# A one-token decode block on one core: the same tiles, written engine by engine with its own semaphores

## The chip, the cores and the metric

The kernel runs on one core of a Trainium2 chip. The metric is the device time of one execution in microseconds (us); less is better. The core has TensorE (PE, matrix products), VectorE (DVE), ScalarE (ACT), GpSimd (POOL) and SyncE (SP, which here issues every DMA), and 16 DMA engines that carry data from HBM into SBUF.

## What is computed

One layer of a transformer decodes one token for two sequences. Attention reads a cache of keys and values; a bilinear feed-forward part follows.

```python
B, Sq, D = 2, 1, 448
H, Sk, Dh = 16, 8192, 256          # heads, cached positions, dims of a head

q = (layernorm(x) @ wq) by heads                     # B, H, 1, Dh
scores = einsum("bhqd,bhkd->bhqk", q, k_cache) * Dh**-0.5
o = einsum("bhqk,bhkd->bhqd", softmax(scores), v_cache)
h = x + o @ wo
n = layernorm(h)
out = h + ((n @ w_gate) * (n @ w_up)) @ w_down       # F = 1792
```

All numbers are float32. The two caches are 2 x 16 x 8192 x 256 numbers each: 32 pairs of a head and a sequence (a *query* below), and for each query 8.39 MB of K and 8.39 MB of V. Each cached number is used once.

## The kernel before

**The work on a query.** `tile_decode_block` is written on a tile framework that places the semaphores: it loops over the 32 queries `i` (L312) in the order in which the program is written. For each it loads K as one tile of 128 partitions x 16384 numbers (`load_k`, L96 to L99) and V as another (`load_v`, L101 to L104). There is one buffer for K and there are two for V; the weight `wq` uses one of V's two first (L106). The scores `s` are four PSUM banks of 128 x 512: a partition group of 32 rows stands for a quarter of the positions.

**Scores, two ways** (`scores`, L253 to L278). The 256 dims of K lie in two halves. In 19 queries TensorE takes both halves, with 32 matmuls at L269. In the other 13 (`by_vector`, L47: every third query and the last three) TensorE takes the lower half with 16 matmuls, VectorE multiplies and adds the upper half (one `tensor_scalar` at L256, then four `scalar_tensor_tensor` at L261, the last two on half the columns each), and TensorE adds its result with 4 matmuls at L275. Then VectorE finds the maximum of each row (L322), and ScalarE makes `p = exp(s - max)` and its sums (L324).

**Values, two ways** (L343 to L352). `WIDE = (8, 8, 0)` says by `i % 3` how many of V's eight slices are taken together. In 19 queries VectorE multiplies all 128 x 16384 numbers of V by `p` (L346) and sums them (L347); in 13 it runs one `scalar_tensor_tensor` with a running sum on each of eight slices (L350).

**After the loop.** The softmax of a query is done piece by piece on 128 partitions, and `weights` (L280) works out the factors that put the pieces together: for the first 30 queries at the end of query 29, for the last two while the last V is on its way. `weigh` (L305) applies them. Then come the output projection (`project_out`, L390), the layer norm, the gate and up products (`project_ff`, L435), their product, the down projection (`add`, L460), two copies to SBUF and one DMA out (L477). The weights for this are loaded behind the last V through the same buffers: `wo` (L359), then gate, up and down in pieces (L366).

**What sets the order.** Every engine runs its instructions in the order of the program. SP's list is `wq`, K0, V0, K1, V1 and so on to V31 and then the weights; a DMA is issued when its buffer is free, and all of them share one queue. K(i+1) waits until TensorE and VectorE have read K(i). The framework has eight semaphores for DMA landings and uses them in turn. At its end (L541) it makes SP wait for every last count, joins all engines in a barrier, clears the semaphores on GpSimd and joins them again.

Of the kernel before, what the change touches and what calls it, by code (L numbers as in the profile page):

```python
# [1 line left out]

# [6 lines left out]
F32 = mybir.dt.float32  # L9
# [5 lines left out]
EPS = 1e-5  # L15
P = 128
HALF = 64
DC = 4
# [23 lines left out]


WIDE = (8, 8, 0)


def by_vector(i):  # L47
    return i % 3 == 0 or i >= NQ - 3

# [6 lines left out]

@with_exitstack
def tile_decode_block(  # L60
    ctx: ExitStack,
    tc: tile.TileContext,
    kc: bass.AP,
    vc: bass.AP,
    wq: bass.AP,
    wo: bass.AP,
    wg: bass.AP,
    wu: bass.AP,
    wd: bass.AP,
    out: bass.AP,  # L70
):

    nc = tc.nc
    const = ctx.enter_context(tc.tile_pool(name="const", bufs=1))
    kbuf = ctx.enter_context(tc.tile_pool(name="kbuf", bufs=1))
    vbuf = ctx.enter_context(tc.tile_pool(name="vbuf", bufs=2))
    one = ctx.enter_context(tc.tile_pool(name="one", bufs=1))
    work = ctx.enter_context(tc.tile_pool(name="work", bufs=2))  # L90
    ps_s = ctx.enter_context(tc.tile_pool(name="ps_s", bufs=1, space=bass.MemoryType.PSUM))
    ps_m = ctx.enter_context(tc.tile_pool(name="ps_m", bufs=2, space=bass.MemoryType.PSUM))
    ps_1 = ctx.enter_context(tc.tile_pool(name="ps_1", bufs=1, space=bass.MemoryType.PSUM))
    ctx.enter_context(tc.manual_schedule())

    def load_k(b, h):  # L96
        t = kbuf.tile([P, 2, G, GK], F32, tag="k", align_bytes=512, name=f"k_{h}_{b}")
        nc.sync.dma_start(t.rearrange("p c g k -> p (c g k)"), kc[b, h])  # L98
        return t  # L99

    def load_v(b, h):  # L101
        t = vbuf.tile([P, NO, GK], F32, tag="v", align_bytes=512, name=f"v_{h}_{b}")
        nc.sync.dma_start(t.rearrange("p o k -> p (o k)"), vc[b, h])
        return t  # L104

    wq_t = vbuf.tile([P, WQ + DC * B], F32, tag="v", align_bytes=512, name="wq_t")  # L106
    nc.sync.dma_start(wq_t, wq)  # L107

    ident = const.tile([P, P], F32, name="ident")
    make_identity(nc, ident)  # L110
    ones = const.tile([P, P], F32, name="ones")
    nc.gpsimd.memset(ones, 1.0 / R)
    eps_t = const.tile([P, 1], F32, name="eps_t")
    nc.gpsimd.memset(eps_t, EPS)
    gsum = const.tile([P, R], F32, name="gsum")
    xr = const.tile([P, DC + 1, B, 16], F32, name="xr")
    nc.gpsimd.memset(xr[:, DC - 1 :], 0.0)
    oT = const.tile([P, H, 2, B], F32, name="oT")
    block = const.tile([P, P], F32, name="block")
    nc.gpsimd.memset(block, 0.0)  # L120
    for g in range(G):
        nc.gpsimd.memset(block[g * R : (g + 1) * R, g * R : (g + 1) * R], 1.0)
    nm = const.tile([P, NQ], F32, name="nm")
    ls = const.tile([P, NQ], F32, name="ls")
    oacc = const.tile([P, NQ, NO], F32, name="oacc")
    acc_ps = ps_1.tile([P, D], F32, name="acc_ps")

    def clear(t):
        nc.scalar.activation(
            t, eps_t[: t.shape[0]].to_broadcast([t.shape[0], t.shape[1]]), AF.Copy, scale=0.0  # L130
        )

    clear(acc_ps)

    def over_chunks(t, tag):

        got = const.tile([P, B], F32, name=f"sum_{tag}")
        nc.vector.tensor_reduce(  # L138
            got, t[:, : DC - 1].rearrange("p c b -> p b c"), axis=AX.X, op=ALU.add
        )  # L140
        nc.vector.scalar_tensor_tensor(  # L141
            got, t[:, DC - 1, :], 0.5, got, op0=ALU.mult, op1=ALU.add
        )
        return got

    def center(h, tag):
        total = ps_m.tile([P, B], F32, tag="sm", name=f"total_{tag}")
        nc.tensor.matmul(total, ones, over_chunks(h, f"h_{tag}"), start=True, stop=True)  # L148
        if h.space == bass.MemoryType.PSUM:
            stays = const.tile([P, DC, B], F32, name=f"stays_{tag}")  # L150
            nc.scalar.activation(stays, h, AF.Copy)
            h = stays
        xc = const.tile([P, DC, B], F32, name=f"xc_{tag}")
        nc.vector.scalar_tensor_tensor(
            xc, total[:, None, :].to_broadcast([P, DC, B]), -R / D, h, op0=ALU.mult, op1=ALU.add
        )
        return xc

    def squares(xc, tag):
        sq = const.tile([P, DC, B], F32, name=f"sq_{tag}")  # L160
        nc.vector.tensor_mul(sq, xc, xc)
        return over_chunks(sq, f"sq_{tag}")

    xT = const.tile([P, DC, B], F32, name="xT")
    nc.scalar.activation(xT, wq_t[:, WQ:].rearrange("p (c b) -> p c b", c=DC), AF.Copy)  # L165
    xc = center(xT, "x")
    var = ps_m.tile([P, B], F32, tag="sm", name="var_x")
    nc.tensor.matmul(var, ones, squares(xc, "x"), start=True, stop=True)
    std = const.tile([P, B], F32, name="std")
    nc.scalar.activation(std, var, AF.Sqrt, bias=eps_t, scale=R / D)  # L170
    rstd = const.tile([P, B], F32, name="rstd")
    nc.vector.reciprocal(rstd, std)

    def spread_out(xc, by):

        for (rows, c, to), copy in zip(LAYOUT, by):
            k = rows.stop - rows.start
            copy(
                xr[rows, to],
                xc[rows, c][:, :, :, None].to_broadcast([k, c.stop - c.start, B, 16]),  # L180
            )

    def scalar_copy(to, x):
        nc.scalar.activation(to, x, AF.Copy)  # L184

    xn = const.tile([P, DC, B], F32, name="xn")
    nc.vector.tensor_mul(xn, xc, rstd[:, None, :].to_broadcast([P, DC, B]))
    spread_out(xn, (scalar_copy,) * 3)
    nc.vector.tensor_reduce(
        gsum, ident.rearrange("p (g r) -> p r g", r=R), axis=AX.X, op=ALU.add  # L190
    )

    def project(ps, w, size, wide, at0, at3):
        for c in range(DC):
            for g in range(4):
                xs = xr[:, c]
                at = c * size + at0[g]
                if c == DC - 1:
                    xs = xr[:, c + g % 2]
                    at = 3 * size + at3[g]  # L200
                nc.tensor.matmul(  # L201
                    ps[32 * g : 32 * g + 32, : wide[g]],
                    xs.rearrange("p b r -> p (b r)"),
                    w[:, at : at + wide[g]], start=(c == 0), stop=(c == DC - 1),
                )

    qT = const.tile([P, 2, G, 2, 2, B], F32, name="qT")
    q_ps = ps_s.tile([P, 4, MM], F32, tag="s", name="q_ps")
    q_sb = one.tile([P, 3, MM], F32, tag="p", name="q_sb")
    spread = q_sb[:, 2].rearrange("p (o g r) -> p o g r", o=G, g=G)  # L210
    nc.gpsimd.tensor_copy(
        spread,
        ident.rearrange("p (o r) -> p o r", r=R)[:, :, None, :].to_broadcast([P, G, G, R]),
    )
    for k in range(2):
        project(
            q_ps[:, k], wq_t, HD, (MM,) * 4, [k * BATCH + g * MM for g in range(4)],
            [k * BATCH // 2 + (g // 2) * MM for g in range(4)],
        )
        nc.scalar.activation(q_sb[:, k], q_ps[:, k], AF.Copy, scale=DH**-0.5)  # L220
        for n in range(4):
            nc.tensor.transpose(
                q_ps[:, 2 + k, n * P : (n + 1) * P], q_sb[:, k, n * P : (n + 1) * P], ident
            )
        nc.scalar.activation(
            qT[:, k].rearrange("p g j c b -> p (j c) g b"),
            q_ps[:, 2 + k].rearrange("p (n g b r) -> p n g b r", n=4, g=G, b=B)[..., 0],
            AF.Copy,
        )


    qd = const.tile([P, G, NQ], F32, name="qd")
    qd_ps = ps_m.tile([P, G, NQ], F32, tag="sm", name="qd_ps")
    for o in range(G):
        nc.tensor.matmul(
            qd_ps[:, o, :].rearrange("p (n b) -> p n b", b=B),
            spread[:, o].rearrange("p g r -> p (g r)"),
            qT.rearrange("p k g j c b -> p (k g j) c b")[:, :, 1, :],
            start=True, stop=True,
        )  # L240
    nc.scalar.activation(qd, qd_ps, AF.Copy)

    def queries(h):
        q = one.tile([P, 2, B, R], F32, tag="q", name=f"q_{h}")
        nc.scalar.activation(  # L245
            q.rearrange("p c b r -> p (c b) r"),
            qT.rearrange("p k g j c b -> p (k g j) (c b)")[:, h, :, None]
            .to_broadcast([P, 2 * B, R]),
            AF.Copy,
        )  # L250
        return q

    def scores(s, q, i, kt):  # L253
        upper = kt[:, 1]
        if by_vector(i):
            nc.vector.tensor_scalar(  # L256
# [288 lines left out]
```

## Time and profile before

| | us |
|---|---|
| median of 3 runs | 1303.92 |
| lowest and highest | 1303.84, 1303.94 |
| span of the profiled execution (first to last instruction) | 1302.1 |

The page gives no time of its own for the profiled execution beyond its span. The median of the runs is 1.8 us longer; that is what lies around the span, ahead of the first instruction and behind the last. The profiled execution's own time is therefore taken as 1302.1 + 1.8 = 1303.9.

How to read the rows. A row of a timeline says when something starts, how long it takes, on which engine, at which line, what it writes and reads, and in brackets how long the engine sat idle before it and what ended that. SPq rows are DMA issues; the transfer itself comes later. PE rows with "x32" may be fewer matmuls in the program: each float32 matmul is two passes there. PEclk is TensorE's granted clock as a share of 2.4 GHz.

### The profile page before, as it was taken

To read this page: it belongs to the slowest core of one execution; us is meant where nothing else is said; L and a number is where in the kernel's file an instruction comes from. 1 tells how busy PE (TensorE), PEld (TensorE's weight loads), DVE (VectorE), ACT (ScalarE), POOL (GpSimd) and SP (SyncE) were. 2 spreads that over 40 slices of the span, in tenths; PEclk is the share of its full clock that TensorE was granted. 3 is DMA by queue.
4 is the path that set the end of the run, shared out by engine and by line. 5 is a ranking of instruction groups with operands and counts; after the bars stand their busy time and mean duration, and the time that the engine had idled before them with its cause. 6 is when DMAs were issued, how large, how long until landed. Compare 5 with 4: busy or idle time off the path is not lost.

```text
span 1302.1 us, 5034 instructions
## 1 busy us (share of the span) xinstructions
PE 340.6 (26%) x2114; PEld 103.4 (8%) x2114; DVE 1075.6 (83%) x381; ACT 80.4 (6%) x111; POOL 2.2 (0%) x15
## 2 busy tenths in 40 slices
PE   2422112232202223211322311322311232221247
PEld 0100000000000000000000000000000000000013
DVE  0499879969987998899799879979987996987773
ACT  1100000000000000000000000000000000000000
POOL 0000000000000000000000000000000000000000
PEclk9866566666556666556666556666656666656668
DMA  9999999999999999999999999999999999999998
GB/s 419 419 449 421 447 423 445 425 443 427 439 429 441 425 441 427 437 428 437 433 435 433 434 435 435 435 433 437 431 439 431 437 429 435 433 433 433 433 425 358
DMA packets 11401, 561.50 MB, mean 431 GB/s; under 512 B 1266, under 2 KB 1652, under 8 KB 2292
## 3 DMA queue, kind: packets, MB, share of 16 engines
q1 hardware_dynamic: 11380, 561.20, 99.6%
q8 instruction: 16, 0.26, 0.1%
q14 instruction: 5, 0.04, 0.0%
HBM read 561.19 MB, written 0.00 MB: 431 GB/s over the span
## 4 chain that ended last, share of the span: by engine, by line
DMA 73%; PE 17%; DVE 10%; issue 1%; SPq 0%; DVEq 0%; ACT 0%; ACTq 0%
DMA k<-in_kc_dram 67%; PE s L269 13%; DVE k L261 6%; DMA v<-in_vc_dram 4%; PE s L275 3%; DVE v L350 3%; DMA wd_t<-in_wd_dram 2%; DVE k L256 1%; PE acc_ps L462 0%; SPq L366 0%; SPq L107 0%; PE u_ps L462 0%; SPq L98 0%; DVEq L256 0%; ACT tail L184 0%
## 5 line engine op out<-in xcount | busy, mean ns | idle before, releaser
L269 PE MATMUL s<-k,q 128*32 128x512 f32 x1632 | 248.3, 773 | 892.5 <-DMA k<-in_kc_dram 892.5
L346 DVE TENSOR_TENSOR v<-v,p 128x16384 f32<-128x16384 f32 x19 | 327.3, 17226 | 81.2 <-DMA v<-in_vc_dram 61.2
L347 DVE TENSOR_REDUCE oacc<-v 128x8 f32<-128x16384 f32 x19 | 327.2, 17220 | 0.7
L350 DVE SCALAR_TENSOR_TENSOR v<-v,p 128x2048 f32<-128x2048 f32 x104 | 231.1, 2288 | 31.8 <-ACT p L324 21.9
L269 PEld LDWEIGHTS s<-k,q 128*32 128x32 f32 x1632 | 66.7, 138 | 1070.9 <-issue 1069.2
L324 ACT ACTIVATE p<-s,nm 128x2048 f32<-128x2048 f32 x32 | 63.0, 1967 | 1131.7 <-DVE nm L322 1131.7
L322 DVE TENSOR_REDUCE nm<-s 128x1 f32<-128x2048 f32 x32 | 73.1, 2285 | 33.8 <-PE s L275 33.8
L261 DVE SCALAR_TENSOR_TENSOR k<-k,qd 128x2048 f32<-128x2048 f32 (+1 forms) x52 | 93.4, 1817 | 1.4
L275 PE MATMUL s<-k,block 128*128 128x512 f32 x104 | 48.1, 605 | 18.1 <-DVE k L261 18.1
L256 DVE TENSOR_SCALAR k<-k,qd 128x2048 f32<-128x2048 f32 x13 | 16.7, 1286 | 29.2 <-DMA k<-in_kc_dram 27.0
L275 PEld LDWEIGHTS s<-k,block 128*128 128x128 f32 x104 | 18.7, 189 | 49.0 <-DVE k L261 33.5
L138 DVE TENSOR_REDUCE sum_h_x<-xT 128x2 f32<-128x6 f32 x1 | 0.2, 159 | 20.6 <-ACT xT L165 20.6
L395 PE MATMUL acc_ps<-wo_t,oT 128*2 128x448 f32 x64 | 8.8, 646 | 11.4 <-DMA wo_t<-in_wo_dram 11.2
L201 PE MATMUL q_ps<-wq_t,xr 128*32 128x512 f32 x64 | 9.6, 753 | 1.4 <-ACT xr L184 1.1
L350 DVE DVE_READ_ACCUMULATOR v<-v,p 128x1 f32 x104 | 8.6, 83 | 0.0
L201 PE MATMUL ff_ps<-gu_t,xr 128*32 128x512 f32 (+1 forms) x32 | 6.4, 913 | 0.6 <-ACT xr L184 0.6
L324 ACT ACTIVATION_READ_ACCUMULATOR p<-s,nm 128x1 f32 x32 | 6.2, 193 | 0.0
L148 PE MATMUL total_x<-sum_h_x,ones 128*128 128x2 f32 x2 | 0.6, 348 | 21.1 <-DVE sum_h_x L141 21.1
L442 DVE TENSOR_SCALAR ve<-var_h 128x1 f32<-128x1 f32 x1 | 0.2, 158 | 6.4 <-PE var_h L440 6.4
L476 DVE COPY tail<-acc_ps 2x112 f32<-2x112 f32 x1 | 0.3, 261 | 5.5 <-PE acc_ps L462 5.5
L245 ACT ACTIVATE q<-qT 128x128 f32<-128x128 f32 x16 | 4.8, 298 | 0.0
L201 PE MATMUL u_ps<-gu_t,xr 128*32 128x512 f32 (+1 forms) x32 | 3.6, 544 | 0.0
(103 smaller groups left out, 66.0 us busy)
## 6 DMA issues: line engine op xcount, KB each, us to landing
wq_t<-in_wq_dram SPq DMA_DIRECT2D x1, 7172.0 KB, 19.6
wo_t<-in_wo_dram SPq DMA_DIRECT2D x1, 3584.0 KB, 16.5
wo_t<-in_wo_dram SPq DMA_DIRECT2D x1, 2688.0 KB, 22.5
gu_t<-in_B_w_gate_dram SPq DMA_DIRECT2D x1, 1792.0 KB, 28.0
gu_t<-in_B_w_up_dram SPq DMA_DIRECT2D x1, 1792.0 KB, 34.5
gu_t<-in_B_w_gate_dram SPq DMA_DIRECT2D x1, 1344.0 KB, 30.7
wd_t<-in_wd_dram SPq DMA_DIRECT2D x1, 1120.0 KB, 16.8
wo_t<-in_wo_dram SPq DMA_DIRECT2D x1, 896.0 KB, 24.2
```

The lines of the kernel that those rows point to most:

```text
L201: nc.tensor.matmul(ps[32 * g : 32 * g + 32, : wide[g]], xs.rearrange("p b r -> p (b r)"), w[:, at : at + wide[g]], start=(c == 0), stop=(c ...
L245: nc.scalar.activation(q.rearrange("p c b r -> p (c b) r"), qT.rearrange("p k g j c b -> p (k g j) (c b)")[:, h, :, None] .to_broadcast([P ...
L256: nc.vector.tensor_scalar(upper[:, 0], upper[:, 0], qd[:, 0, i : i + 1], None, op0=ALU.mult)
L261: nc.vector.scalar_tensor_tensor(upper[:, 0, at], upper[:, o, at], qd[:, o, i : i + 1], upper[:, 0, at], op0=ALU.mult, op1=ALU.add,)
L269: nc.tensor.matmul(s[g * R : (g + 1) * R, at], q[:, c, i % B, :], kt[:, c, g, at], start=(c == 0), stop=(c == 1), skip_group_check=True,)
L275: nc.tensor.matmul(s[:, at], block, upper[:, 0, at], start=False, stop=True, skip_group_check=True,)
L322: nc.vector.tensor_reduce(nm[:, i : i + 1], s, axis=AX.X, op=ALU.max, negate=True)
L324: nc.scalar.activation(p, s, AF.Exp, bias=nm[:, i : i + 1], scale=1.0, accum_out=ls[:, i : i + 1])
L346: nc.vector.tensor_mul(v, v, p[:, None, :].to_broadcast([P, n, GK]))
L347: nc.vector.tensor_reduce(oacc[:, i, :n], v, axis=AX.X, op=ALU.add)
L350: nc.vector.scalar_tensor_tensor(v, v, 1.0, p, op0=ALU.mult, op1=ALU.mult, accum_out=oacc[:, i, o : o + 1])
L395: nc.tensor.matmul(acc_ps[32 * j : 32 * j + B, :], oT[:, h, c, :], wo_t[:, k * D : (k + 1) * D], start=(h < 2 and j > 0), stop=(h >= H - 2 ...
```

## The change

The kernel is written again without the tile framework. Tiles are placed by hand at fixed addresses, each engine's list of instructions is written out, and the semaphores are the kernel's own. In front of and behind the loop a small class (`Flow`) keeps the last writer and the readers of each tile and emits a wait for each dependence. In the loop the waits are written by hand.

- **One form for all 32 queries.** VectorE always takes the upper half of K's dims, TensorE the lower; V is always taken in eight slices. The L346 and L347 forms are gone. The pieces, tiles and PSUM banks are as before, and so are all bytes loaded.
- **GpSimd hands landings over.** It waits for K's landing and increments `k_for_pe` and `k_for_dve`; it waits for V's and increments `v_for_dve`. TensorE and VectorE wait for these and set them back to zero (`take`). GpSimd also copies the query (`q_now`, `qd_now`) ahead of each K, and the eight sums of V (`oacc_now`) away behind each V. ScalarE copies the maximum away.
- **When K's buffer is taken again.** SP issues K(i+1) when VectorE has found the maximum of query i (`n_max`).
- **The end.** `weights` is done once for all 32 queries, between the eight slices of the last V; each load has a semaphore of its own; the matmuls that bring in `x` (L385) move ahead of the loop.
- **No closing barriers.** SP issues the output, clears the semaphores, and waits for the output's landing; nothing joins the engines.

```diff
+    def take(e, name):
+        f.engines[e].wait_ge(sem[name], 1).then_inc(sem[name], -1)
+
+    def pe_scores():
+        take("pe", "k_for_pe")
         for at in tiles:
...
+        for j, at in enumerate(tiles):
+            if j % 2 == 0:
+                take("pe", "part")
+            last = pe.matmul(
+                s[:, at], block, k_t[:, 1, 0, at], start=False, stop=True, skip_group_check=True
             )
+        last.then_inc(sem["scored"], 1)
...
+    def dve_scores():
+        take("dve", "k_for_dve")
...
+        take("dve", "scored")
+        dve.tensor_reduce(nm_now, s, axis=AX.X, op=ALU.max, negate=True).then_inc(sem["n_max"], 1)
...
+    def dve_values(j):
+        take("dve", "v_for_dve")
+        take("dve", "p_ready")
+        for o in range(NO):
+            last = mix(v_t[j], o, oacc_now[:, o : o + 1])
+        last.then_inc(sem["n_v"], 1)
...
+    def hand_k(i, copied):
+        f.wait("pool", copied, (sem["k_in"], 16 * (i + 1)))
+        pool.sem_inc(sem["k_for_pe"], 1)
+        pool.sem_inc(sem["k_for_dve"], 1)
...
+    def pool_steps():
+        copied = queries(0)
+        f.wait("pool", pe_ready)
+        for i in range(NQ):
+            hand_k(i, copied)
+            if i:
+                copied = keep(i - 1)
+            if i < NQ - 1:
+                f.wait("pool", copied, v_in(i))
+                pool.sem_inc(sem["v_for_dve"], 1)
+                copied = queries(i + 1)
+                f.wait("pool", (sem["n_exp"], i + 1))
...
+    def load_k(i):
+        if i:
+            f.wait("sp", (sem["n_max"], i))
...
+    def load_v(i, *after):
+        if i > 1:
+            f.wait("sp", (sem["n_v"], i - 1))
...
+    f.wait("sp", *ends[2:])
+    sp.dma_start(out.rearrange("b s d -> (b s) d"), y).then_inc(first, 16)
+    last = nc.alloc_semaphore("past")
+    sp.sem_clear(range(first.num + 1, last.num))
+    sp.wait_ge(first, 16).then_inc(first, -16)
...
-    with _tile.TileContext(nc) as tc:
-        tile_decode_block(tc, *args)
+    decode_block(nc, *args)
```

**VectorE, the second query and the third, before** (`nm` is the maximum, `v` the values, `p` the exponentials; names in brackets are semaphores, DMAHW those of landings):

```order
L322 TENSOR_REDUCE nm<-s_229 128x1 [waits PE_49]
L346 TENSOR_TENSOR v_1_227<-v_1_227,p_263 128x16384 [waits DMAHW4_49,DMAHW0_49,Activation_49]
L347 TENSOR_REDUCE oacc<-v_1_227 128x8 [waits DVE_49]
L322 TENSOR_REDUCE nm<-s_273 128x1 [waits PE_49]
L350 SCALAR_TENSOR_TENSOR v_0_271,oacc<-v_0_271,p_307 128x2048 [waits DMAHW6_49,Activation_49]
L350 SCALAR_TENSOR_TENSOR v_0_271,oacc<-v_0_271,p_307 128x2048 x7
```

The same engine now, for every query:

```order
L428 TENSOR_SCALAR k_t<-k_t,qd_now 128x2048 [waits k_for_dve]
L433 SCALAR_TENSOR_TENSOR k_t<-k_t,qd_now 128x2048 [waits step] x2
L433 SCALAR_TENSOR_TENSOR k_t<-k_t,qd_now 128x1024 [waits step] x2
L440 TENSOR_REDUCE nm_now<-s 128x1 [waits step,scored]
L443 SCALAR_TENSOR_TENSOR v_t_51,oacc_now<-v_t_51,p 128x2048 [waits v_for_dve,p_ready]
L443 SCALAR_TENSOR_TENSOR v_t_51,oacc_now<-v_t_51,p 128x2048 x7
```

The two queries that ran without a share of K on VectorE now have one; the wide pair of instructions is gone, and landings are waited for through GpSimd's semaphores.

**VectorE from the last maximum on, before** (`low` to `rl` are steps of `weights`):

```order
L322 TENSOR_REDUCE nm<-s_1539 128x1 [waits PE_49]
L286 TENSOR_REDUCE low_1570<-nmT_1568 2x1 [waits PE_49]
L288 TENSOR_SCALAR diag_1572<-ident,low_1570 2x2 [waits DVE_49]
L292 SCALAR_TENSOR_TENSOR w_1576<-all_ps_1574,nm 128x2 [waits PE_49]
L297 TENSOR_TENSOR lw_1579<-ls,w_1576 128x2 [waits Activation_49]
L301 RECIPROCAL rl_1583<-l_ps_1581 128x2 [waits PE_49]
L302 TENSOR_TENSOR w_1576<-w_1576,rl_1583 128x2 [waits DVE_49]
L350 SCALAR_TENSOR_TENSOR v_1_1537,oacc<-v_1_1537,p_1566 128x2048 [waits DMAHW0_49]
L350 SCALAR_TENSOR_TENSOR v_1_1537,oacc<-v_1_1537,p_1566 128x2048 x7
L306 TENSOR_TENSOR oacc<-oacc,w_1576 128x16 [waits DVE_49]
```

And now (L583 is `weigh`, for the first 30 queries):

```order
L443 SCALAR_TENSOR_TENSOR v_t_51,oacc<-v_t_51,p 128x2048 [waits p_ready,n_exp,v_in1]
L555 TENSOR_REDUCE low<-sm 32x1 [waits n_pe]
L557 TENSOR_SCALAR diag<-ident,low 32x32 [waits n_dve]
L443 SCALAR_TENSOR_TENSOR v_t_51,oacc<-v_t_51,p 128x2048
L567 SCALAR_TENSOR_TENSOR w<-sm,nm 128x32 [waits n_pe]
L574 TENSOR_TENSOR lw<-ls,w 128x32 [waits n_act]
L579 RECIPROCAL rl<-sm 128x32 [waits n_pe]
L580 TENSOR_TENSOR w<-w,rl 128x32 [waits n_dve]
L583 TENSOR_TENSOR oacc<-oacc,w 128x240 [waits n_pool,n_dve]
L443 SCALAR_TENSOR_TENSOR v_t_51,oacc<-v_t_51,p 128x2048 x4
L583 TENSOR_TENSOR oacc<-oacc,w 128x16 [waits n_dve,n_pool]
```

The steps of `weights` stood ahead of the last V's slices and now stand between them (two more slices stand ahead of L574 and L579), and `weigh` for the first 30 queries comes here too.

**SP, the loads of the last query and the first weights, before:**

```order
L98 DMA k_1_1535<-in_kc_dram 128x16384 [waits DMAHW5_49,DVE_49,PE_49]
L103 DMA v_1_1537<-in_vc_dram 128x16384 [waits DMAHW4_49]
L359 DMA wo_t<-in_wo_dram 128x7168 [waits DMAHW7_49,DVE_49,PE_49]
L359 DMA wo_t<-in_wo_dram 128x5376
L359 DMA wo_t<-in_wo_dram 128x1792
```

The same now, and below it GpSimd's instructions of one query, which had none before (its other steps are waits and increments, which this view leaves out):

```order
L182 DMA k_t<-in_kc_dram 128x16384 [waits n_max]
L189 DMA v_t_51<-in_vc_dram 128x16384 [waits n_v]
L104 DMA wo_t<-in_wo_dram 128x7168 [waits n_max]
...
L476 COPY oacc<-oacc_now 128x8 [waits k_in,n_exp,n_pool,n_v]
L462 COPY q_now<-qT 128x32 [waits n_pool,v_in1,n_max]
L466 COPY qd_now<-qd 128x4 [waits n_pool]
```

The order of the loads is the same; K's load waits for the maximum and no longer for TensorE's last matmul.

## Rows read from the trace of the kernel before

**Rows 1.** The page: span, busy time of the engines, DMA queues, chain that ended last.
```profile
span 1302.1 us, 5034 instructions
...
PE 340.6 (26%) x2114; PEld 103.4 (8%) x2114; DVE 1075.6 (83%) x381; ACT 80.4 (6%) x111; POOL 2.2 (0%) x15
...
q1 hardware_dynamic: 11380, 561.20, 99.6%
q8 instruction: 16, 0.26, 0.1%
...
DMA 73%; PE 17%; DVE 10%; issue 1%; SPq 0%; DVEq 0%; ACT 0%; ACTq 0%
```

**Rows 2.** Busy time by stage; the last three columns are PEclk, DMA share, GB/s.
```profile
39.70:1240.40 1200.70, 289.17 (x1703) 83.56 (x1704) 1040.66 (x329) 68.89 (x83) 0.00 (x0) 0.63 1.00 434
```

**Rows 3.** Timeline from the end of query 29 through query 30 (narrow forms).
```profile
1200.23 0.41 DVE L306 TENSOR_TENSOR oacc<-oacc,w 128x240 f32<-128x240 f32 x1
1201.70 1.29 DVE L256 TENSOR_SCALAR k<-k,qd 128x2048 f32<-128x2048 f32 x1 [1.06 <-DMA k<-in_kc_dram]
...
1212.87 0.33 SPq L98 DMA_DIRECT2D k<-in_kc_dram  x1
1212.87 2.29 DVE L322 TENSOR_REDUCE nm<-s 128x1 f32<-128x2048 f32 x1 [2.60 <-PE s L275]
...
1215.26 1.97 ACT L324 ACTIVATE p<-s,nm 128x2048 f32<-128x2048 f32 x1 [36.14 <-DVE nm L322]
...
1221.07 2.29 DVE L350 SCALAR_TENSOR_TENSOR v<-v,p 128x2048 f32<-128x2048 f32 x1 [5.91 <-DMA v<-in_vc_dram]
...
1238.77 0.08 DVE L350 DVE_READ_ACCUMULATOR v<-v,p 128x1 f32 x1
1240.37 1.28 DVE L256 TENSOR_SCALAR k<-k,qd 128x2048 f32<-128x2048 f32 x1 [1.51 <-DMA k<-in_kc_dram]
```

**Rows 4.** Groups by line and shape: the wide form of V, and GpSimd's only copy.
```profile
L346 DVE TENSOR_TENSOR v<-v,p 128x16384 f32<-128x16384 f32 x19 | 327.3, 17226 | 81.2 <-DMA v<-in_vc_dram 61.2 <-ACT p L324 20.0
...
L211 POOL COPY q_sb<-ident 128x512 f32<-128x512 f32 x1 | 0.6, 609 | 0.1
```

**Rows 5.** The end of the program: SP's wait there, and GpSimd's rows of L541.
```profile
SPq L541 <- DMA out_dram<-tail: 0.6, 1, 0.6
...
L541 POOLq EVENT_SEMAPHORE  x4: 17/17/17, 1301.4 to 1302.0; - x4
```

**Rows 6.** Busy time of VectorE alone (count) in query 29's steps of `weights`.
```profile
1176.60:1182.20 5.60, 1.47 (x7) 0.73 1.05 456
```

**Rows 7.** Timeline of the tail, from V31's landing to the output's issue.
```profile
1259.63 2.29 DVE L350 SCALAR_TENSOR_TENSOR v<-v,p 128x2048 f32<-128x2048 f32 x1 [2.30 <-DMA v<-in_vc_dram]
...
1268.12 4.74 PE L395 MATMUL acc_ps<-wo_t,oT 128*2 128x448 f32 x32 [9.53 <-DMA wo_t<-in_wo_dram]
...
1274.48 3.17 PE L395 MATMUL acc_ps<-wo_t,oT 128*2 128x448 f32 x28 [1.62 <-DMA wo_t<-in_wo_dram]
...
1279.24 0.62 DVE L412 COPY tail<-acc_ps 128x448 f32<-128x448 f32 x1 [1.09 <-PE acc_ps L395]
...
1282.67 6.44 PE L201 MATMUL ff_ps<-gu_t,xr 128*32 128x512 f32 x32 [0.62 <-ACT xr L184]
...
1289.35 3.63 PE L201 MATMUL u_ps<-gu_t,xr 128*32 128x512 f32 x32
...
1295.04 0.26 PE L462 MATMUL acc_ps<-wd_t,hmT 128*2 128x112 f32 x2
...
1298.95 0.09 PEld L462 LDWEIGHTS acc_ps<-wd_t,hmT 128*2 128x2 f32 x4 [0.21 <-DMA wd_t<-in_wd_dram]
...
1300.02 0.33 SPq L477 DMA_DIRECT2D out_dram<-tail  x1
```

**Rows 8.** Stretches of the tail: PE and PEld busy (count); PEclk is third from the end.
```profile
1282.60:1288.30 5.70, 5.63 (x30) 2.27 (x32) 0.36 (x3) 0.54 (x2) 0.00 (x0) 0.50 0.99 420
...
1296.40:1297.40 1.00, 0.95 (x32) 0.68 (x32) 1.00 0.57 224
```

## Prediction before the run

> **What bounds the kernel now.** I read the page's DMA queues first: SP's queue moves 561.20 MB and keeps the 16 DMA engines busy for 99.6% of the span, while VectorE, the busiest engine, has 83% [rows 1]. The table by stage says the same of the loop alone: from K0's landing to K31's the DMA share is 1.00 at 434 GB/s [rows 2]. A query has 16.78 MB, which at 434 GB/s takes 38.66 us, and K30 and K31 land 1201.70 and 1240.37, 38.67 apart [rows 3]. So the loop runs at the pace of the transfers, and 561.20 MB at 434 GB/s are 1293.1 of the 1302.1 us. The chain names TensorE with 17% and VectorE with 10% [rows 1], but that is only who freed K's buffer; K31 was issued at 1212.87 and had to stand in the queue until V30 had landed, at 1221.07 [rows 3]. The issue was 8.2 us early. An engine's time counts only where that 8.2 us is used up, or where no transfer is left: at the very end.
>
> What a change can win is thus some 9 us ahead of the first byte and behind the last. 0.2% of the time, 2.6 us, is about what a measurement of this kernel can tell from no change; below 1301.3 is faster, above 1306.5 slower.
>
> **The change part by part.** The bytes, their order and the pieces are unchanged, so the 1293.1 us of transfers stay.
>
> *One form for all queries.* Query 30 already has the form that all get, so its rows price it [rows 3]: K's landing to the last matmul 11.17 us (1201.70 to 1212.87), the maximum 2.29 (to 1215.26 with its hop), the exponentials 1.97 and some 0.2 for their sum, eight slices of V 17.78 (1221.07 to 1238.85). That is 33.5 us of VectorE's chain in a period of 38.67. A wide query had 17.23 us for the product [rows 4], about as much again for the sum, and the maximum, 36.8. VectorE gets more uniform and slightly freer; it bounds neither before nor after. I cost this at 0, and its cover is 5.2 us a query; were it gone, each microsecond over would cost up to 31.
>
> *K's buffer is given back later.* SP now waits for the maximum, 2.29 us behind the last matmul, with V(i+1)'s load queued behind that wait. The 8.2 us of lead become 5.9.
>
> *GpSimd in between.* No row has such a hand-over. The nearest: GpSimd's four barrier steps at the end lie between 1301.4 and 1302.0 [rows 5], so a wait and an increment are some 0.1 to 0.2 us; K's hand-over is one wait and two increments, 0.3 to 0.4 us, V's the same with one. The upper end is a hand-over that also waits for GpSimd's copies; its only copy there, 128 x 512 numbers, took 0.61 us [rows 4], and the copies are much smaller (128 x 32 and less), so two are under 1.2 us. With 0.4 the lead becomes 5.5 us, with 1.6 it is 4.3. A DMA needs some time from its issue to its bytes; the output, 3.6 KB, needed 1.3 us for all of it (issued 1300.02 [rows 7], next barrier step 1301.4 [rows 5]). 3.0 us are left in the worst of these, so the cost is 0, from 0 to 0. Behind GpSimd's wait for V(i) stand the copies of query i+1 and the hand-over of K(i+1), 19.3 us later.
>
> Those copies start just as VectorE starts eight slices that read V and p. The Trainium skill (SBUF — State Buffer, section Who interferes with whom) says that a VectorE instruction with two SBUF inputs and a GpSimd instruction that reads SBUF exclude each other, and that the later one "fully blocks". No run here shows it yet. By that rule the copies stand until VectorE pauses.
>
> In numbers of this kernel: V lands 1221.07, VectorE pauses at 1238.85, two copies of under 0.61 us end by 1240.1, and K31 lands at 1240.37 [rows 3]. Even copies that wait for all eight slices are in time, and 4 us of lead stand behind that. The sum is the same either way.
>
> *Instructions fetched.* 16 blocks of instructions, 0.26 MB, share the DMA engines [rows 1]: 0.1% of 16 x 1302, between 0.7 and 2.0 us of an engine on average. TensorE's list goes from 1064 matmuls to 833, VectorE's grows; I take 0, and for the bound that an engine which is last gets one block less, 16 KB at a sixteenth of 434 GB/s, -0.6 us; two less is -1.2.
>
> *The end of VectorE's list.* Before, V31 lands at 1259.63 and the sum in `acc_ps` is copied at 1279.24 [rows 7], 19.6 us later. Now the eight slices (17.8) carry the steps of `weights` between them (1.47, from query 29 with 30 columns [rows 6]) and `weigh` for 30 queries (0.41 [rows 3]): the last slice ends 19.7 us after the landing, not 17.8. TensorE's first 15 heads of the output projection must wait for that `weigh`: four slices (8.9) + 1.9 + matmul and four copies (1.5) = 12.3; its 60 passes took 4.74 + 3.17 [rows 7], so they end at 20.2. With the last head's 1.6 us the copy comes at 21.9: 2.3 late. From that copy to the first pass of the down projection it was 15.8 us (1279.24 to 1295.04 [rows 7]); that pass moves from 1295.04 to 1297.3. Until then it had waited for weights; now all but the last pieces have landed. Four chunks take 0.95 us when landed [rows 8], fourteen 3.3, so they end at 1300.1 or so, where the old end is 1299.65: +0.45. The bounds come from TensorE's clock. The gate product took 6.44 us, with the granted clock 0.50 (1.2 GHz) for 5.7 of them, and the up product 3.63 at the upper level [rows 7, 8]. If both ran at the upper level, 2.8 us go and the weights' landing sets the end as before: 0. If both ran at the lower, +2.8: +3.3. I take +0.45, since the gate again follows a pause of TensorE in small steps.
>
> *No closing barriers.* SP's wait for the output ends and GpSimd's first barrier step is at 1301.4; its last is at 1302.0 and the span ends at 1302.1 [rows 5, 1]. These 0.8 us go, unless what lies around the span takes the same time to gather the engines: -0.8, between -0.8 and 0.
>
> *Begin.* SP's first load loses a branch: 0 to -0.1, I take 0.
>
> Sum: 1302.1 - 0.8 + 0.45 = 1301.75, and with the 1.8 us around it **1303.5 us**, against 1303.9 for the profiled execution and 1303.92 for the median of the runs: no change that can be told.
>
> **The rivals.** *The tail runs into TensorE's clock.* The mechanism is the one above: 2.3 us late, then the up product at 1.2 GHz, +3.3 in place of +0.45, 1306.4. It decides once the first pass of the down projection comes later than about 1296.9, 1.9 us behind its old place. For it: the chain has no slack by my sum. Against: the up product had the full clock after the gate had kept TensorE busy for 6.4 us. Slower, at the edge of what can be told; 0.14 (0.06 of it above 1306.5).
>
> *A wait takes the place of the one removed.* GpSimd hands K over so late that K(i+1) is issued after V(i) has landed. It decides beyond 3 to 4 us of delay a query, and then each further microsecond costs 31: 1335 for one. It could come of copies blocked behind VectorE; against it, VectorE pauses before K lands [rows 3]. 0.05.
>
> *The closing does not get shorter.* The engines have to be gathered anyway behind the span, and only the name of that time changes: 1303.5 + 0.8 = 1304.3. 0.15.
>
> *Fewer blocks on the last DMA engine and an unharmed tail.* -0.8 - 1.2 = 1301.9. 0.12, of which 0.05 below 1301.3, if the time around the span shrinks too.
>
> **How the numbers follow.** The forecast itself has 0.54. The likeliest time is 1303.5. Its neighbours reach from 1301.9 to 1304.3; on the upper side I go half way to the clock's rival. 1301.8 to 1305.6 leaves out the worst of the tail, the stall, and the small part below, 0.2 together. Faster 0.05; slower 0.06 + 0.05 = 0.11; the rest, 0.84, cannot be told from no change.
>
> **What would show it.** In the profile after: the loop's DMA share stays at 1.00 and 434 GB/s; K's landings stay 38.67 us apart; SP issues K(i+1) about 5.5 us ahead of V(i)'s landing; VectorE waits for both landings in each query; the wide instructions' 654 us are gone and VectorE's busy time falls to about 920 (a query's 11.2 less TensorE's share of 2.6, 2.3 and 17.8, times 32); GpSimd's steps are short. In the tail the copy of `acc_ps` comes some 22 us after V31, and the passes of the down projection run on without waiting for `wd`. The span ends with the landing of the output. The prediction is wrong if DMA idles between transfers in the loop, if the tail from V31's landing to the output's issue is off 40.8 us by more than 1.5, or if the time around the span is not 1.8.

## The result, and the profile after

The changed kernel takes **1306.41 us** (median of 19 runs, 1305.66 to 1307.73), the kernel before 1303.94 (19 runs, 1303.55 to 1304.56): a ratio of 1.0019, 95% interval 1.0013 to 1.0026. It is slower by 2.5 us (0.2%), and lies above the range of the prediction. The profiled execution took 1305.77 us, with a span of 1304.4, so 1.4 us lie around it.

The page of the changed kernel, the lines that answer to [rows 1], and one more queue:

```profile
span 1304.4 us, 4776 instructions
...
PE 343.7 (26%) x1653; PEld 110.6 (8%) x1653; DVE 920.3 (71%) x736; ACT 80.2 (6%) x126; POOL 80.0 (6%) x110
...
q1 hardware_dynamic: 11380, 561.20, 99.6%
q8 instruction: 13, 0.21, 0.1%
q14 instruction: 11, 0.09, 0.0%
```

VectorE is busy for 920.3 us, as forecast (920), but it has 736 instructions where it had 381. TensorE's blocks of instructions (q8, 16 KB each) fell from 16 to 13. The blocks of 8 KB (q14) rose from 5 to 11. The prediction used q8's row alone; q14's row in the page of the kernel before is this:

```profile
q14 instruction: 5, 0.04, 0.0%
```

The loop by the table of stages, from K0's landing to K31's, which answers to [rows 2]:

```profile
39.70:1243.41 1203.71, 291.51 (x1246) 89.98 (x1248) 885.01 (x682) 67.42 (x94) 76.97 (x93) 0.64 1.00 433
```

The DMA share is still 1.00, and the loop still lasts 3.0 us longer. A share rounded to two places cannot show 3 us in 1200. Query 30 in the timeline, answering to [rows 3]:

```profile
1203.80 1.29 DVE L428 TENSOR_SCALAR k_t<-k_t,qd_now 128x2048 f32<-128x2048 f32 x1 [1.60 <-DVEq L406]
...
1215.15 2.29 DVE L440 TENSOR_REDUCE nm_now<-s 128x1 f32<-128x2048 f32 x1 [2.77 <-DVEq L406]
1217.47 0.33 SPq L182 DMA_DIRECT2D k_t<-in_kc_dram  x1
...
1222.92 0.21 POOL L462 COPY q_now<-qT 128x32 f32<-128x32 f32 x1 [18.96 <-DMA v_t<-in_vc_dram]
...
1223.43 2.29 DVE L443 SCALAR_TENSOR_TENSOR v_t<-v_t,p 128x2048 f32<-128x2048 f32 x1 [5.99 <-DVEq L406]
...
1241.13 0.08 DVE L443 DVE_READ_ACCUMULATOR v_t<-v_t,p 128x1 f32 x1
1243.41 1.29 DVE L428 TENSOR_SCALAR k_t<-k_t,qd_now 128x2048 f32<-128x2048 f32 x1 [2.19 <-DVEq L406]
```

VectorE waits for both landings and has time to spare, as forecast; the lead of K31's issue to V30's landing is some 5 us (issued at 1217.47; GpSimd's first copy behind V30 starts at 1222.92), also as forecast. Yet K30 and K31 are 39.6 us apart, not 38.67. The tail, answering to [rows 7]:

```profile
1262.39 2.29 DVE L443 SCALAR_TENSOR_TENSOR v_t<-v_t,p 128x2048 f32<-128x2048 f32 x1 [5.34 <-DMA v_t<-in_vc_dram]
...
1284.77 0.62 DVE L655 COPY tail<-acc_ps 128x448 f32<-128x448 f32 x1 [1.02 <-PE acc_ps L611]
...
1288.35 6.07 PE L698 MATMUL s<-gu_t,xr 128*32 128x512 f32 x32 [0.82 <-DVE sum_sq_h L243]
...
1294.66 3.63 PE L698 MATMUL u_ps<-gu_t,xr 128*32 128x512 f32 x32
...
1302.55 0.26 DVE L788 COPY tail<-acc_ps 2x112 f32<-2x112 f32 x1 [3.43 <-PE acc_ps L760]
...
1303.18 0.33 SPq L794 DMA_DIRECT2D out_dram<-tail  x1
```

So the difference of the two profiled executions divides like this: V31 lands at 1262.39 instead of 1259.63, **+2.76**; from there to the output's issue 40.79 us instead of 40.39, +0.40; from the issue to the end of the span 1.26 instead of 2.06, -0.8; around the span 1.37 instead of 1.82 (with the time that was taken for the execution before), -0.45. Sum +1.9. The median of the runs is another 0.6 above the profiled execution.

**Where the 2.76 come from.** Each transfer is carried by all 16 DMA engines, and its landing in the trace is 16 events, one by each engine. Below, for some of K's transfers, the first, the next to last and the last of the 16, in us behind a grid on which K(i) is due at 39.00 + 38.64 i; e7, e9 and e10 are experiments told below.

| | K2 | K12 | K21 | K31 |
|---|---|---|---|---|
| before | 0.01 / 0.66 / 1.65 | 0.12 / 1.81 / 2.08 | 0.15 / 2.95 / 3.12 | 0.13 / 3.20 / 3.43 |
| changed | 0.27 / 1.22 / 1.59 | 0.38 / 2.88 / 3.34 | 1.61 / 4.05 / 4.54 | 3.07 / 4.53 / 6.21 |
| e7 | 0.06 / 1.29 / 1.75 | 0.12 / 2.22 / 2.95 | 0.09 / 2.11 / 4.62 | 0.72 / 3.39 / 6.27 |
| e9 | 0.07 / 1.14 / 1.65 | 0.20 / 1.82 / 1.86 | 0.21 / 2.03 / 3.55 | 0.18 / 3.16 / 4.32 |
| e10 | 0.19 / 1.32 / 1.76 | 0.22 / 1.96 / 3.83 | 0.24 / 1.99 / 6.37 | 2.71 / 4.49 / 8.03 |

The DMA engines do not keep step: a block of instructions holds one of them, the others go on, and a landing waits for the last. In the changed kernel two things are seen. One engine falls behind by some 0.8 us at a time, at 104, 298, 492, 664, 842, 1033 and 1227 us: seven of the eleven 8-KB blocks start there. Such a block takes its engine 0.31 us, and the engine's next packet of 64 KB takes 2.95 us instead of 2.42: 0.83 us in all. The trace does not name the engine of a packet, but an engine's next packet starts 4 ns before the one ahead of it ends, so its packets can be followed: all seven blocks are on one engine. Before, three of the five were (at 259, 723 and 1149 us). TensorE's 16-KB blocks go round: those of e2 hit eight engines in turn.

And the engines that are ahead lose their lead too: the first is 3 us late at K31. In the changed kernel K's issue is only 2.1 to 4.1 us ahead of the *first* engine to finish V (mostly 5.3 ahead of the last), and wherever that is under 2.8 us, and in a few queries with more, the first packets of K take longer, up to 4.1 us.

Hence two theories of the +2.5 us, and a rival from the prediction. **A, late issue:** K's buffer comes free at the maximum, and DMA engines run dry. **D, VectorE's list:** its instructions come in blocks through one and the same DMA engine, and more of them make that engine the last. **B:** GpSimd's hand-over costs. In the expectations of e1 to e4 D is still called C, and C also takes in accidents of the DMA engines.

### The profile page after: what moved, and what is told of

The parts are those of the page before. It is cut to its first block, busy times and chain, and to the rows that moved or that the text cites. A ratio compares the mean times of both kernels' runs of the same rounds, so it can differ in the third digit from the quotient of the medians.

```text
span 1304.4 us, 4776 instructions
## 1 busy us (share of the span) xinstructions
PE 343.7 (26%) x1653; PEld 110.6 (8%) x1653; DVE 920.3 (71%) x736; ACT 80.2 (6%) x126; POOL 80.0 (6%) x110
## 5 line engine op out<-in xcount | busy, mean ns | idle before, releaser
L443 DVE SCALAR_TENSOR_TENSOR v_t<-v_t,p 128x2048 f32<-128x2048 f32 x256 | 569.2, 2286 | 181.6 <-DVEq L406 176.3
L412 PE MATMUL s<-k_t,q_now 128*32 128x512 f32 x1024 | 182.3, 877 | 851.6 <-PEq L406 851.6
L433 DVE SCALAR_TENSOR_TENSOR k_t<-k_t,qd_now 128x1024 f32<-128x1024 f32 (+1 forms) x128 | 229.9, 1817 | 3.4
L440 DVE TENSOR_REDUCE nm_now<-s 128x1 f32<-128x2048 f32 x32 | 73.3, 2292 | 90.5 <-DVEq L406 90.5
L419 PE MATMUL s<-k_t,block 128*128 128x512 f32 x256 | 119.1, 608 | 61.8 <-PEq L406 61.8
L496 ACT ACTIVATE p<-s,nm_now 128x2048 f32<-128x2048 f32 x32 | 62.9, 1967 | 1150.0 <-DVE nm_now L440 1150.0
L412 PEld LDWEIGHTS s<-k_t,q_now 128*32 128x32 f32 x1024 | 46.2, 154 | 983.5 <-issue 983.5
L428 DVE TENSOR_SCALAR k_t<-k_t,qd_now 128x2048 f32<-128x2048 f32 x32 | 41.2, 1286 | 66.9 <-DVEq L406 66.9
L466 POOL COPY qd_now<-qd 128x4 f32<-128x4 f32 x32 | 64.9, 2027 | 3.2 <-ACT qd L388 1.3
L419 PEld LDWEIGHTS s<-k_t,block 128*128 128x128 f32 x256 | 46.7, 192 | 137.8 <-issue 137.7
```

The source lines that it names most:

```text
L412: pe.matmul(s[g * R : (g + 1) * R, at], q_now, k_t[:, 0, g, at], start=True, stop=False, skip_group_check=True,)
L419: last = pe.matmul(s[:, at], block, k_t[:, 1, 0, at], start=False, stop=True, skip_group_check=True)
L428: dve.tensor_scalar(upper[:, 0], upper[:, 0], qd_now[:, 0:1], None, op0=ALU.mult).then_inc(step, 1)
L433: got = dve.scalar_tensor_tensor(upper[:, 0, at], upper[:, o, at], qd_now[:, o : o + 1], upper[:, 0, at], op0=ALU.mult, op1=ALU.add,)
L440: dve.tensor_reduce(nm_now, s, axis=AX.X, op=ALU.max, negate=True).then_inc(sem["n_max"], 1)
L443: return dve.scalar_tensor_tensor(v[:, o], v[:, o], 1.0, p, op0=ALU.mult, op1=ALU.mult, accum_out=to)
```

## The experiments

The lists below count VectorE's instructions as built, with semaphore steps, and one more for each running sum. Landings are those of the last DMA engine. The kernel before was timed again beside each group of runs (e1 to e4, e5 to e8, e9 to e11); its medians were 1303.93, 1303.92 and 1303.95, so times of different groups can be compared.

| | VectorE's list | K's issue waits for | K31 | V31 | median us (lowest to highest) |
|---|---|---|---|---|---|
| before | 434 | matmul | 1240.27 | 1259.60 | 1303.94 (1303.55 to 1304.56) |
| changed | 902 | maximum | 1243.05 | 1262.37 | 1306.41 (1305.66 to 1307.73) |
| e1 | 870 | matmul | 1242.18 | 1261.52 | 1305.48 (1305.17 to 1305.84) |
| e2 | 814 | matmul | 1242.07 | 1261.37 | 1305.69 (1305.56 to 1306.15) |
| e3 | 846 | after maximum | 1242.67 | 1262.47 | 1306.82 (1306.49 to 1307.58) |
| e4 | 902 | exponentials | 1272.17 | 1291.52 | 1335.68 (1331.66 to 1344.04) |
| e5 | 1265 | matmul, but late | 1245.57 | 1265.88 | 1311.11 (1310.05 to 1314.32) |
| e6 | 814 | matmul | 1242.18 | 1261.48 | 1305.71 (1305.52 to 1305.88) |
| e7 | 902 | matmul | 1243.11 | 1262.43 | 1305.86 (1305.08 to 1306.82) |
| e8 | 743 | maximum | 1241.89 | 1261.19 | 1304.83 (1304.29 to 1305.85) |
| e9 | 743 | matmul | 1241.16 | 1260.47 | 1304.41 (1304.31 to 1304.76) |
| e10 | 1265 | matmul | 1244.87 | 1265.15 | 1309.42 (1309.26 to 1309.49) |
| e11 | 382 | matmul | 1240.44 | 1259.77 | 1302.79 (1302.44 to 1304.78) |

**e1: K's buffer from the last matmul.**

```diff
-            f.wait("sp", (sem["n_max"], i))
+            f.wait("sp", (sem["scored"], i))
...
-        take("dve", "scored")
+        dve.wait_ge(sem["scored"], i + 1)
```

> The changed kernel with one thing put back: SP takes K's buffer from TensorE's last score matmul, not from VectorE's maximum. Theory A (late issue): in the changed kernel K and V of the next query are issued only 1.8 to 2.8 us before the first of the 16 DMA engines has finished V, so the engines that are ahead run dry, and their first K packets take up to 4.1 us instead of 2.42. Here the issue is 2.3 us earlier, so no K packet is lengthened but those beside an instruction block, K31 and V31 land some 2.8 us earlier, the time is 1303.2 to 1304.2 and the runs lie closer together. Theory B (hand-over by GpSimd is what costs) and theory C (more instruction blocks, or accidents of the DMA engines): 1306.4 as before, within 0.5.

1305.48: a third of what A asked for. The first packets of K were no longer lengthened, but for a few queries, most of them near the end, and the first DMA engine stayed within 0.8 us of its pace; the last engine was still 5.3 us behind. The edit also took one semaphore step a query out of VectorE's list, and at K31 six blocks had come, not seven. A alone does not explain it, and the run mixes two causes. (The lead of 1.8 to 2.8 us in the expectation is 2.1 to 4.1 by the landings.)

**e2 and e3: the form alone, then K kept through the maximum**, both on the kernel before.

```diff
-WIDE = (8, 8, 0)
+WIDE = (0, 0, 0)
...
-    return i % 3 == 0 or i >= NQ - 3
+    return True
```

> The kernel before with the form alone: all queries get half of K's dims by VectorE, and V's slices in one instruction each; K's buffer is free at TensorE's last matmul, no GpSimd between. Theory A (late issue): the issue lies 4.7 us or more ahead of the first DMA engine that is done, as in the queries of that form before, so nothing is lost: 1303.5 to 1304.5. Theory C (VectorE's list or the form itself brings instruction blocks or traffic that disturb the DMA engines): 1305.5 to 1306.5.

```diff
         nc.vector.tensor_reduce(nm[:, i : i + 1], s, axis=AX.X, op=ALU.max, negate=True)
+        nc.vector.tensor_copy(kept, kt[:, 1, 0, :1])
```

> The run e2_one_form with one small VectorE read of K behind each maximum, so that K's buffer comes free some 2.4 us later, as in the changed kernel, but without GpSimd. Theory A (late issue): +1.5 to +3.5 us against e2_one_form, with lengthened first K packets once the DMA engines are over 1.5 us apart: 1305 to 1307.5. Theories B and C: within 0.5 of e2_one_form.

The form alone costs 1.75 us, with no GpSimd, no own semaphores and no late issue. B cannot explain that, nor can A. The page of e2:

```profile
PE 346.2 (27%) x1658; PEld 110.4 (8%) x1658; DVE 921.8 (71%) x742; ACT 80.4 (6%) x111; POOL 2.2 (0%) x15
...
q14 instruction: 8, 0.07, 0.0%
```

e3 adds 1.13 us to that, and its runs do not overlap with e2's. Its 32 small reads bring no further block ahead of V31 (six of VectorE's in both), so the late issue does cost something, less than A had said.

**e4: K's buffer still later** (`n_exp` in place of `n_max` in SP's wait).

> The changed kernel with K's buffer taken from ScalarE's copy behind the exponentials, some 2.2 us after the maximum. Theory A (late issue): the first DMA engine is done about 0.5 us after the issue, so in nearly every query engines run dry; the loss per query is larger than the changed kernel's 0.09 us: 1309 to 1335. Theories B and C: 1306.4, within 0.7.

1335.68, beyond the upper end. The issue came about 1.1 us ahead of the first DMA engine, 674 packets of 64 KB took over 2.5 us (81 in the changed kernel), and the loop moved 422 GB/s:

```profile
39.68:1272.20 1232.52, 291.92 (x1240) 90.81 (x1240) 885.02 (x682) 67.27 (x94) 76.86 (x92) 0.63 0.99 422
```

So A's mechanism is real: an issue some 2 us later than the changed kernel's costs 29 us.

**e5, e6 and e10: 480 small instructions more, on VectorE, on ScalarE, and on VectorE in another place.** All on e2; the first two stand behind V's slices, the third behind the maximum. e6 has `scalar_copy` in place of `nc.vector.tensor_copy`.

```diff
+        if i < EARLY:
+            for _ in range(16):
+                nc.vector.tensor_copy(pad, eps_t)
```

> The run e2_one_form with 16 one-element VectorE copies behind V's slices of each of the first 30 queries, where VectorE has 5 us to spare; K's issue, the bytes and the form stay. Theory D (VectorE's instruction list): its blocks of 8 KB all come through one and the same DMA engine, each holds that engine for 0.83 us (0.30 idle, 0.53 on the packet behind), the others don't wait for it and the landing does; 480 instructions are 3.75 blocks more: +2.5 to +3.3 us against e2_one_form's 1305.7, so 1308.2 to 1309.0, with V31 landing as much later. Theory A (late issue) and theory B (hand-over): 1305.7, within 0.3. If only the bytes counted, 30 KB over 16 engines: +0.1.

> The same 480 small instructions, but on ScalarE, whose list is short. Theory D, if each engine's blocks come through a DMA engine of its own: as many blocks as in e5_vector_pad, but on a DMA engine that is ahead, so it only loses its lead: 1305.3 to 1306.3, no more than 0.6 from e2_one_form. If blocks cost wherever they are fetched, or if ScalarE's and VectorE's come through the same DMA engine: 1308 to 1309, as in e5_vector_pad.

> e5_vector_pad again with its flaw mended: the 16 copies took 3.0 us and stood between V's slices and K's product, where VectorE has 1.5 us to spare, so K's issue came up to 4 us late. Here they stand behind the maximum, where VectorE waits 5 us for V; K's issue stays 8 us ahead of V's last landing. Theory D: 3.75 blocks more than e2_one_form on VectorE's DMA engine, +2.5 to +3.3: 1308.2 to 1309.0, the other 15 engines where they were. Theories A and B: 1305.7, within 0.3.

e6 costs nothing (1305.71 against e2's 1305.69), with as many 8-KB blocks as e10. The two pages, e6 and then e10:

```profile
PE 342.8 (26%) x1658; PEld 108.8 (8%) x1658; DVE 921.8 (71%) x742; ACT 174.4 (13%) x591; POOL 2.2 (0%) x15
...
q14 instruction: 12, 0.10, 0.0%
```

```profile
PE 344.8 (26%) x1658; PEld 109.0 (8%) x1658; DVE 992.4 (76%) x1222; ACT 80.5 (6%) x111; POOL 2.2 (0%) x15
...
q14 instruction: 12, 0.10, 0.0%
```

e10 takes 1309.42, +3.73 against e2, with V31 3.78 later. D had said 2.5 to 3.3 and is right in kind and a little low. The list grew by 451, as some waits fell away, and ten of VectorE's blocks start ahead of V31 where e2 has six: four times 0.83 are 3.3. The rest may come of this, which no run shows by itself: a last engine that is further behind also holds back K's landing, and so the issue, while the others run on; their lead falls to 2.0 us, and some run dry. The bytes are the same in e6 and e10; what counts is whose list it is. Five of e6's blocks come 271 us apart and are ScalarE's; followed packet by packet they are all on one engine too, but on another than VectorE's. The last engine of e6 stands at K31 where e2's does (5.34 and 5.23 behind the grid). What the expectation of e5 calls 0.30 us idle is the block's own transfer. e5 was a poor experiment: its copies took 3.0 us where VectorE had 1.5 to spare, K's issue came up to 4 us late, and its +5.4 has both causes in it.

**e7, e8 and e9: the two causes apart.** e7 is e1 with VectorE's list at its full length:

```diff
-            f.wait("sp", (sem["n_max"], i))
+            f.wait("sp", (sem["scored"], i))
...
-        take("dve", "scored")
+        dve.wait_ge(sem["scored"], i + 1).then_inc(sem["past_scores"], 1)
```

> The changed kernel with K's buffer taken from TensorE's last matmul as in e1_k_at_matmul, but with VectorE's list at its full length (a semaphore step stays in the place of the one that e1 lost). Theory D alone: 7 blocks as in the changed kernel, 1306.1 to 1306.7. Theory A alone: 1303.5 to 1304.2. Both (the blocks set the engine that is last, the late issue adds to it in some of the runs): 1305.5 to 1306.0, and the runs lie within 1 us where the changed kernel's lie within 2.

e8 keeps the late issue and shortens the list; e9 is both.

```diff
-        take("dve", "k_for_dve")
+        dve.wait_ge(sem["k_for_dve"], i + 1)
...
-            dve.wait_ge(step, n)
+            dve.wait_ge(step, 3 * i + n)
...
-        dve.wait_ge(step, 3).then_inc(step, -3)
-        take("dve", "scored")
+        dve.wait_ge(sem["scored"], i + 1)
...
-        take("dve", "v_for_dve")
-        take("dve", "p_ready")
+        dve.wait_ge(sem["v_for_dve"], i + 1)
```

> The changed kernel with 5 semaphore steps a query less in VectorE's list: waits on counts that only rise, joined to the instruction behind them, and GpSimd also waits for the exponentials before it hands V over. K's buffer still comes free at the maximum. VectorE's list goes from some 900 instructions (each sum of a slice counts as one more) to some 740, so 5 blocks in the loop where there were 7. Theory D: 1.7 us less, 1304.4 to 1305.1. Theory A: the issue is at most 0.2 us earlier, so 1306.0 to 1306.5.

> The run e8_lean with K's buffer taken from TensorE's last matmul, so both shorter list and early issue. Theory D alone (VectorE's blocks set the DMA engine that is last; the late issue only costs engines that are ahead of it): 1304.5 to 1305.1, as e8_lean, the DMA engines that are ahead staying within 1 us of their first pace. Theory A adding its share: 1303.8 to 1304.4.

e7's time lies in the range of both causes together, though its runs spread over 1.7 us and not 1; e8's is D's; e9's lies at the edge between D alone and A adding its share. At K21 of e7 no engine but one is late (table above: next to last 2.11, last 4.62), and that one lands K31 and V31 just where the changed kernel does, 1243.11 and 1262.43. In these two profiled executions the late issue thus costs nothing: it held engines that were ahead anyway. Over the runs e7 is 0.55 lower than the changed kernel, and e9 0.42 lower than e8. The shorter list is worth 1.58 with the late issue (e8) and 1.45 with the early one (e9, whose runs lie below all of e7's). The runs of the changed kernel, e3 and e8, with the late issue, spread over 1.1 to 2.1 us, e9's over 0.45; e7's spread over 1.7, and there the lead to the first engine fell to 2.3 us as well.

**e11: the new frame with the old forms.** e9 with the kernel before's `by_vector` and `WIDE`, so that VectorE's list is short again:

```diff
+        if not by_vector(i):
+            for at in tiles:
+                for c in range(2):
...
+        if wide(i):
+            v = v_t[j]
+            dve.tensor_mul(v, v, p[:, None, :].to_broadcast([P, NO, GK])).then_inc(sem["step"], 1)
...
+            dve.tensor_reduce(oacc_now, v, axis=AX.X, op=ALU.add).then_inc(sem["n_v"], 1)
```

> The changed kernel's frame (own semaphores, no closing barriers, GpSimd hands over, the tail) with the kernel before's two forms of a query: wide products of V and K by TensorE alone where it had them. VectorE's list falls to some 390 instructions, 3 blocks, as before; K's buffer from TensorE's last matmul. Theory D: the landings come as before (K31 at 1240.4, V31 at 1259.6, within 0.5), and what is left of the change is its end: closing -0.8, around the span -0.45, the tail +0.25 to +0.45: 1302.7 to 1303.4. Theory B (hand-over) or a cost of the frame that we do not know: 1304.5 or more.

1302.79, as D said, with the landings of the kernel before. It is the fastest of all, 1.2 us below the kernel before by the medians, but the ratio is 0.9993 with an interval of 0.9984 to 1.0002: no difference that can be told. Two of its 11 runs lie above 1303.9, and its profiled one has 2.6 us around a span of 1301.4; why is open.

## Why the prediction was wrong

- **What bounds the kernel:** right. The loop runs at the pace of the transfers, and VectorE's 920 us were forecast to the microsecond. But that pace was taken as fixed, with K's landings 38.67 us apart; it also hangs on the instruction blocks.
- **The step that failed is "Instructions fetched", taken as 0 with bounds of -0.6 and -1.2 us.** It measured +2.8: V31 lands 2.76 us later, and e7 lands it just as late without the late issue. Three things were wrong in it. It read one queue of instruction blocks, TensorE's, and not the one behind it. For its bound it did look at the engine that is last, but it priced a block by its bytes (0.6 us for 16 KB, where an 8-KB block of VectorE's costs 0.83) and did not ask whether blocks fall on the same engine. And it saw that VectorE's list grows, but not by how much: 381 busy instructions to 736. The form that makes VectorE *less busy* has twice the instructions: the wide form had 2 for V where the narrow one has 8 and 8 sums. e1's blocks were 194 us apart, 5.0 queries of some 26 instructions, so about 130 fill a block; with 0.83 us a block, 468 instructions more are worth 3.0 us by this estimate. e10 (up), e8 and e9 (down), e11 (back to the old landings) and e6 (no effect from ScalarE) show the cause.
- **"K's buffer is given back later", 0 to 0:** its lead was right (5.3 us, forecast 5.5), its bound was not. The lead was counted to the last DMA engine's landing; the first engine had only 2.1 to 4.1 us. What it cost the changed kernel is 0 in the profiled execution and about 0.5 us over the runs, where the ranges of e7 and the changed kernel overlap; that share is probable, not shown. e3 and e4 show that it can cost.
- **GpSimd in between, 0:** right. K31 lands at 1243.05 and VectorE starts at 1243.41; before, 1240.27 and 1240.37, so the hand-over adds about 0.3 us. In 29 of the 32 queries GpSimd's second copy starts 0.12 us after VectorE's first slice and takes 2.2 us, while the larger copy ahead of it takes 0.2:

```profile
L466 POOL COPY qd_now<-qd 128x4 f32<-128x4 f32 x32 | 64.9, 2027 | 3.2 <-ACT qd L388 1.3
L462 POOL COPY q_now<-qT 128x32 f32<-128x32 f32 x32 | 6.7, 211 | 625.5 <-DMA v_t<-in_vc_dram 591.4
```

The Trainium skill (SBUF — State Buffer, section Who interferes with whom) says that of a VectorE instruction with two SBUF inputs and a GpSimd instruction that reads SBUF the later one is blocked. By that rule, the trace agrees. The prediction had the copies stand until VectorE pauses; here the wait lasts for one VectorE instruction (2.29 us), not for all eight slices. Off the path, as forecast.
- **The tail, +0.45:** measured +0.40, but luck is in that. By the prediction's own terms the passes of the down projection end at 1297.3 + 3.3 = 1300.6, not 1300.1, and the term should have been +0.95. The copy of `acc_ps` comes 22.4 us behind V31 (forecast 21.9); the first of those passes came 37.3 us behind it (forecast 37.7), and they ran on, in 2.9 us instead of 3.3. The up product kept the full clock with 3.63 us, so the clock's rival did not come; that the time of its case, 1306.4, is the one measured is chance.
- **No closing barriers, -0.8:** measured -0.8, and the rival that the closing does not get shorter fell. Not forecast was another -0.45 around the span. In e1, e7, e8 and e9, which have no barriers either, 1.3 to 1.4 us lie there; in e2 and e6, which have them, 1.8; the profiled execution of e11, with its 2.6, does not fit. That the time around the span would not be 1.8 is the one of the prediction's signs of being wrong that plainly came.
- **Fewer blocks:** this rival had looked at the right thing with the wrong sign. TensorE's blocks did become fewer, but VectorE's on the last engine became more.

## What to carry to other kernels

Where a kernel is bound by DMA, count the instructions of each engine's list and look at every queue of instruction blocks. Here VectorE's blocks all fell on one DMA engine, and each landing waited for that one. Fewer and wider instructions can be worth more than a less busy engine, and semaphore steps count like any other (e8 and e9). Measure the lead of an issue against the first DMA engine to run dry, not against the landing of the transfer ahead.

## What was not expected of the hardware

- An 8-KB block of VectorE's instructions costs its DMA engine 0.83 us though its own transfer takes 0.31; as many blocks more, but for ScalarE, cost the kernel nothing (e6).
- VectorE's blocks all come through one DMA engine, ScalarE's in e6 through another, TensorE's through eight in turn.
- The 16 DMA engines drift apart in the course of a run, by 3.3 us at K31 before and by 5.6 in e7, with a DMA share of 1.00 in the loop. In the changed kernel it is 3.1, with the last 6.2 behind the grid, because the late issue holds the first ones back too.
- In e11 GpSimd's copy of 128 x 64 numbers stands for the whole of VectorE's wide product (17.23 us), and the next copy is free again:

```profile
447.38 17.23 DVE L478 TENSOR_TENSOR v_t<-v_t,p 128x16384 f32<-128x16384 f32 x1 [2.16 <-POOLq L523]
447.46 17.24 POOL L495 COPY q_now<-qT 128x64 f32<-128x64 f32 x1 [4.19 <-ACT p L530]
...
464.76 0.19 POOL L499 COPY qd_now<-qd 128x4 f32<-128x4 f32 x1
```
